# GpSimd's first task of a slot: the split of the probabilities or the integer sum of the lesser scores

## The chip, the cores and the metric

The kernel runs on one core of a Trainium2 chip. The metric is the device time of one execution in microseconds (us). The core has five engines that run their own instruction streams in program order and meet at semaphores: TensorE (PE in the profile; PEld is its loading of weights), VectorE (DVE), ScalarE (ACT), GpSimd (POOL) and the sync engine (SP), which here only issues transfers. Working memory is SBUF, and TensorE's results land in PSUM.

## The reference

Two blocks follow each other. The first is attention that keeps the 32 largest scores of a row; the second is a feed-forward block whose activation is h·cos(h). All is float32.

```python
# q, k, v: (8 batches, 8 heads, 576 tokens, 64)
scores = scale * q @ k.T
kth = np.partition(scores, -32, axis=-1)[..., -32:-31]
scores = np.where(scores >= kth, scores, -1e9)
attn = np.exp(scores - scores.max(-1, keepdims=True))
attn = attn / (attn.sum(-1, keepdims=True) + 1e-9)
x = (attn @ v) as (4608 tokens, 512)
h = x @ w_in            # 512 -> 2048
out = (h * np.cos(h)) @ w_out   # 2048 -> 512
```

## The kernel before

**Units and slots.** The attention is cut into 144 units. A unit is 128 tokens and one pair of heads, so a tile of scores is 128 × 2 × 576. The main loop (line 849) has one slot for each unit, and a slot works on several units at once: `u` is the unit whose largest scores are searched, `w` the one before it (masking and exponentials), `x` the one before that (its probabilities are sent away to be transposed), and `z`, in even slots only, the two units before those, whose probabilities are multiplied with the values. Slots 0 to 8 follow `early_slot`, slots 9 to 140 `slot`, the rest `last_slot`. The order in which the functions are called is the order of the instructions on each engine: it is written by hand, and no scheduler moves anything.

**The search.** VectorE finds the 32 largest of 576 scores with MAX8 (line 349) and MATCH_REPLACE8 (line 354), eight at a time. To halve the work, the row is folded. `fold_high` (VectorE, line 244) takes the larger of each of 288 pairs into `rest`. The lesser of each pair comes from GpSimd: `fold_sum` (line 262) adds the two as integers into `low`, and `fold_low` (line 271) subtracts the larger one. Four rounds search `rest`, and then two rounds search `low`. There is one buffer `low`, so the integer sum of a slot has to wait until the last search of the slot before is over. That search stands at the end of a slot, interleaved with the sum (line 396) and the reciprocal (line 401) of the unit `w`; the reciprocal, `rden`, is VectorE's last instruction in a slot. In this document a slot starts where this reciprocal ends.

**Sending the probabilities.** ScalarE masks and exponentiates the scores of `w` in place (lines 380 and 388). A slot later, `send` (line 739) takes them as `x`. `split` has GpSimd copy the float32 words as two rows of 16-bit halves into the single buffer `halves` (line 421), and then the 16-bit halves of `rden`, 64 times each (line 423). `write_halves` (line 431) writes the buffer to DRAM, and `transposes` (line 437) reads it back transposed as `pT`; both are issued by the sync engine, whose queue also carries the loads of q, k, v and of weights.

**Using them.** In even slots `values` (line 474) has TensorE multiply two units' `pT` with the values. ScalarE copies the result to `xT` (line 481), and `scale_values` (line 493) has VectorE multiply `xT` by the transposed `rden` that came along in `pT`, one instruction for each of the two units. Both inputs of it are in SBUF. It stands ahead of the last search of `low`.

**The feed-forward block** is cut into small steps that are fed in between: products with `w_in` (line 539), the range reduction of the cosine's argument on GpSimd (lines 575 and 584, in even slots), the sine on ScalarE (line 594), the product h·cos(h) on GpSimd (line 601, in odd slots) and products with `w_out` (line 614). In the first slots the weights are also rebuilt from 64-bit input: lines 138 and 151 on GpSimd and line 141 on VectorE.

GpSimd's order in a full slot is thus: lines 262, 421, 423, 271, and then 601 in odd slots or 575 and 584 in even ones.

Of the kernel before, what the change touches and what calls it, by code (L numbers as in the profile page):

```python
# [30 lines left out]
def kernel(  # L31
# [52 lines left out]
    for i in range(DF // CW):  # L84
        w = consts.tile([P, NC, CW], F32, tag=f"w_in{i}", name=f"w_in{i}")
# [4 lines left out]
    for f in range(NF):  # L90
        w = consts.tile([P, DM], F32, tag=f"w_out{f}", name=f"w_out{f}")
# [146 lines left out]
    def fold_high(u):  # L238

        s, sc = u["s"], u["sc"]  # L240
        if u["n"] > EARLY:
            del u["sc"]
        u["rest"] = work.tile([P, 2, S], F32, tag="rest", name="rest", bufs=1)
        nc.vector.tensor_tensor(  # L244
            out=u["rest"][:, :, HS:S], in0=sc[:, :, 0:HS], in1=s[:, :, HS:S], op=ALU.max
        )

    def fold_now(u):

        s, sc = u["s"], u.pop("sc")  # L250
        u["low"] = work.tile([P, 2, HS], F32, tag="low", name="low", bufs=1)
        nc.vector.tensor_tensor(
            out=u["low"], in0=sc[:, :, 0:HS], in1=s[:, :, HS:S], op=ALU.min
        )

    def fold_sum(u):

        if not u["folds"]:
            return
        s = u["s"].bitcast(I32)  # L260
        u["low"] = work.tile([P, 2, HS], F32, tag="low", name="low", bufs=1)
        nc.gpsimd.tensor_tensor(  # L262
            out=u["low"].bitcast(I32), in0=s[:, :, 0:HS], in1=s[:, :, HS:S], op=ALU.add
        )

    def fold_low(u):

        if not u["folds"]:
            return
        low = u["low"].bitcast(I32)  # L270
        nc.gpsimd.tensor_tensor(  # L271
            out=low, in0=low, in1=u["rest"][:, :, HS:S].bitcast(I32), op=ALU.subtract
        )
# [15 lines left out]
    def topk_first(u, w):  # L289

        u["top"] = tops[u["n"] % len(tops)]
        merges = w and w["folds"]
        if merges:
            merge_first(w)
        if u["folds"]:
            if u["n"] > EARLY:
                fold_sum(u)
            fold_high(u)
        else:
            u["rest"] = work.tile([P, 2, S], F32, tag="rest", name="rest", bufs=1)  # L300
        if merges:
            merge_second(w)
        if u["folds"] and u["n"] <= EARLY:
            fold_now(u)
        topk_round(u, 0, [lambda: bounds(w), lambda: distances(w)] if w else ())

    def topk_round(u, rnd, between=(), ahead=None):
        top, rest, lasts = u["top"], u["rest"], TOPK // 8 - 1
        end = TOPK - 1 - 8 * rnd
        at = top[:, :, end : end - 8 if rnd < lasts else None : -1, 0]  # L310
        if u["folds"]:
            search(
                at, rest[:, :, HS:S] if rnd == 0 else rest[:, :, 0:HS], rest[:, :, 0:HS], rnd < lasts,
                between if rnd < lasts else (),
            )
        else:
            search(at, u["s"] if rnd == 0 else rest, rest, rnd < lasts, between)
        if rnd < lasts:
            return
        del u["rest"]  # L320
        if u["folds"]:
            low = u.pop("low")
            for k in range(TOPK // 16):
                more = k < TOPK // 16 - 1
                if ahead and not more:
                    scale_values(ahead)
                search(
                    top[:, :, 1 + 8 * k : 9 + 8 * k, 1], low, low, more,
                    () if more or rnd < lasts else between,
                )  # L330
# [3 lines left out]
    def merge_first(u):  # L334
        n = TOPK // 2 + 1
        u["lesser"] = u["top"].rearrange("p j r i -> p j (r i)")[:, :, 2 * n : 3 * n]
        nc.vector.tensor_reduce(
            out=u["lesser"], in_=u["top"][:, :, 0:n], axis=mybir.AxisListType.X, op=ALU.min
        )

    def merge_second(u):
        nc.vector.tensor_reduce(
            out=u["top"][:, :, TOPK - 1, 1], in_=u.pop("lesser"), axis=mybir.AxisListType.X,
            op=ALU.max,
        )
# [10 lines left out]
    def bounds(u):  # L356

        top = u.pop("top").rearrange("p j r i -> p j (r i)")
        end = 2 * TOPK
        if not u["folds"]:  # L360
            nc.vector.tensor_copy(out=top[:, :, end - 1], in_=top[:, :, 0])
        less = u["less"] = top[:, :, end : end + 2]
        u["near"] = top[:, :, end - 1 : end + 1]
        nc.vector.tensor_reduce(
            out=less, in_=top[:, :, end - 2 : end].unsqueeze(3), axis=mybir.AxisListType.X,
            op=ALU.max, negate=True,
        )

    def distances(u):
        u["nd"] = small.tile([P, 2], F32, tag="nd", name="nd")  # L370
        nc.vector.tensor_reduce(
            out=u["nd"], in_=u.pop("near"), axis=mybir.AxisListType.X, op=ALU.add
        )
# [42 lines left out]
    def split(u):  # L416


        s = u.pop("s").rearrange("p j k -> p (j k)").bitcast(U16)
        halves = work.tile([P, 2, 2 * S + P], U16, tag="halves", name="halves", bufs=1)  # L420
        nc.gpsimd.tensor_copy(out=halves[:, :, 0 : 2 * S], in_=s.rearrange("p (k h) -> p h k", h=2))  # L421
        rden = u.pop("rden").bitcast(U16).rearrange("p (j h) -> p h j", h=2)
        nc.gpsimd.tensor_copy(
            out=halves[:, :, 2 * S :].rearrange("p h (j d) -> p h j d", j=2),
            in_=rden.unsqueeze(3).to_broadcast([P, 2, 2, D]),
        )
        u["halves"] = halves

    def write_halves(u):
        rows = u["rows"] = dram.tile([P, 2, 2 * S + P], U16, tag="rows", name="rows")  # L430
        nc.sync.dma_start(out=rows, in_=u.pop("halves"))

    def transposes(u):
        rows = u.pop("rows").rearrange("q h k -> (q h) k")
        pT = u["pT"] = work.tile([P, 2 * NT + 2, P], F32, tag="pT", name="pT", bufs=3)
        words = pT.rearrange("p c q -> p (c q)").bitcast(U16)
        nc.sync.dma_start_transpose(
            out=words.rearrange("p (c q) -> p c q", c=2 * NT + 2), in_=rows
        )
# [121 lines left out]
    def take_banks():  # L561
        while full:
            take, *what = full.popleft()
            take(*what)
# [22 lines left out]
    def sines(least):  # L587

        n = sum(c[3] < ff["now"] for c in waiting)
        if n == 0 or (n < least and waiting[0][3] + 2 > ff["now"]):  # L590
            return
        for _ in range(n):
            blk, g, x, _ = waiting.popleft()
            nc.scalar.activation(out=x, in_=x, func=AF.Sin, bias=halfpi, scale=TWO_PI_BELOW)  # L594
            sined.append((blk, g, x))
# [143 lines left out]
    def send(x):  # L739

        split(x)
        write_halves(x)
        transposes(x)

    def slot(i, u, w, x, z):
        load_weights(2)
        topk_first(u, w)
        if x:
            send(x)
        fold_low(u)  # L750
        topk_round(u, 1)
        topk_round(u, 2)
        made = scored.get(i, [])
        if z:
            take_banks()
        feed(1)

        ahead = i < EARLY + 5 * NP
        if z and not ahead:
            values(z)  # L760
        for m in made:
            scores(m)
        if z and ahead:
            values(z)


        late = len(made) > 0

        decoding = i < EARLY + 8
        if i % 2 and not decoding:  # L770
            sines(1)
        if w:
            mask(w)
        take_banks()
        if w and late:
            exponentials(w)
        if z and not ahead:
            take_values(z)
        take_scores(units[i + 1])
        if z and ahead:  # L780
            take_values(z)
        if w and not late:
            exponentials(w)
        decode_second(2)
        topk_round(u, 3, both(w), z)
        for load, b, hp in at_slot.get(i, []):
            load(b, hp)
        gate(1)
        feed(1 if len(made) == 2 else 2)
        take_banks()  # L790
        decode_third()
        decode_first(2)
        reduce_first()
        reduce_second()
        feed(1 if len(made) == 2 else 3)
        if decoding or i == LAST:
            sines(1)
# [51 lines left out]
    for i in range(NU + 1):  # L849
# [4 lines left out]
        u, w = (units[i - n] if 0 <= i - n < NU else None for n in range(2))  # L854
# [55 lines left out]
```

## Time and profile before

| what | value |
|---|---|
| time, median of 3 runs | 1515.53 us (1513.83 to 1517.55) |
| span of the profiled execution | 1510.3 us |
| granted TensorE clock, mean of the span | 0.972 |
| GpSimd, integer sum L262, each of 133 | 1413 ns |
| GpSimd, split L421, each of 132 | 2106 ns |
| GpSimd, rden copy L423, each of 132 | 406 ns |
| GpSimd, subtraction L271, each of 133 | 1415 ns |
| GpSimd, range reduction L575 and L584, each of 68 | 1050 ns and 2363 ns |
| VectorE, scaling of the values L493, each of 132 | 476 ns |
| issue to landing, rows written | 3.0 us |
| issue to landing, transposes | 5.1 us |

Durations are means of one instruction, and the two landings are medians. The page gives for every group of instructions the time that its engine was busy with it, the mean of one, and how long the engine stood idle just before, with the instruction that ended the idle time. Idle time of an engine costs nothing by itself. What matters is whether another engine, in the end, stood waiting for it.

### The profile page before, as it was taken

Reading aid. Unit: us, or ns where it says so; the run is one execution under the profiler, and the core shown is the slowest. Engines: PE = TensorE matmul, PEld = TensorE weight load, DVE = VectorE, ACT = ScalarE, POOL = GpSimd, SP = SyncE. Lnnn points to the kernel's source line nnn. Section 1 sums busy time; section 2 is a strip of 40 time slices with the busy share of each in tenths; the row PEclk is TensorE's granted clock in tenths of the full one; section 3 lists DMA queues with packets and bytes.
Section 4 is the critical chain, followed back from the end, with each engine's and each line's share of the span. In section 5 each row is a group of like instructions: output and inputs, shape, how many; then the busy total and the mean of one; then the engine's idle time right before and its main releaser. Section 6 shows DMA issues by size and latency. Waiting matters only on the chain.

```text
span 1510.3 us, 30568 instructions
## 1 busy us (share of the span) xinstructions
PE 1414.7 (94%) x10360; PEld 1014.2 (67%) x10360; DVE 1392.2 (92%) x5209; ACT 1093.4 (72%) x1974; POOL 1157.2 (77%) x836
## 2 busy tenths in 40 slices
PE   4778799999999999999999999999999999999999
PEld 3556567766777766766667767676676766677665
DVE  7999989999999999999999999999899999999831
ACT  4667667777777777777777777777677776777641
POOL 4779878888888887888888888888788888888410
PEclk6689999999999999999999999999999999999999
DMA  8534666567555666556655566557655556645200
GB/s 275 150 106 123 153 183 179 141 161 194 162 160 144 158 189 167 154 143 187 178 151 141 147 188 166 159 147 192 161 163 148 146 155 170 160 135 146 78 8 14
DMA packets 405549, 229.54 MB, mean 152 GB/s; under 512 B 355088, under 2 KB 371728, under 8 KB 405392
## 3 DMA queue, kind: packets, MB, share of 16 engines
q1 hardware_dynamic: 399984, 217.93, 53.2%
q10 hardware_dynamic: 5408, 9.65, 1.8%
q8 instruction: 82, 1.34, 0.4%
q14 instruction: 75, 0.61, 0.1%
HBM read 45.09 MB, written 95.94 MB: 93 GB/s over the span
## 4 chain that ended last, share of the span: by engine, by line
PE 39%; DVE 36%; DMA 10%; ACT 9%; POOL 3%; issue 2%; SPq 1%; ACTq 0%; POOLq 0%
DVE top L349 17%; PE mm L539 14%; PE o L614 13%; DVE rest L354 10%; DMA pT<-rows 7%; PE rim L474 5%; PE sc L223 4%; DVE rest L244 3%; DVE low L354 3%; ACT s L388 2%; DVE xT L493 2%; ACT L388 1%; ACT s L233 1%; PE rim L223 1%; DMA v<-in_v_dram 1%
## 5 line engine op out<-in xcount | busy, mean ns | idle before, releaser
L539 PEld LDWEIGHTS mm<-xT,w_in 128*128 128x128 f32 x4608 | 540.1, 193 | 68.6 <-issue 60.7
L614 PE MATMUL o<-w_out,g 128*128 128x512 f32 x1152 | 541.2, 603 | 12.7 <-POOL g L601 8.8
L539 PE MATMUL mm<-xT,w_in 128*128 128x128 f32 x4608 | 542.8, 276 | 0.9 <-DVE xT L493 0.5
L349 DVE MAX8 top<-rest 128x8 f32<-128x288 f32 x1148 | 481.4, 454 | 0.0
L354 DVE MATCH_REPLACE8 rest<-top,rest 128x288 f32<-128x288 f32 (+1 forms) x860 | 377.1, 446 | 0.0
L262 POOL TENSOR_TENSOR low<-s 128x576 int32<-128x576 int32 x133 | 187.9, 1413 | 214.7 <-DVE rden L401 205.0
L614 PEld LDWEIGHTS o<-w_out,g 128*128 128x128 f32 x1152 | 203.5, 191 | 200.4 <-issue 179.4
L421 POOL COPY halves<-s 128x2304 uint16<-128x2304 uint16 x132 | 277.9, 2106 | 0.1
L349 DVE MAX8 top<-low 128x8 f32<-128x288 f32 x568 | 239.4, 447 | 3.1 <-POOL low L271 3.0
L388 ACT ACTIVATE s<-s,nd 128x576 f32<-128x576 f32 x288 | 220.1, 767 | 0.8
L380 ACT ACTIVATE s<-s,top 128x576 f32<-128x576 f32 x288 | 206.0, 764 | 0.0
L474 PE MATMUL rim<-pT,v 128*64 128x128 f32 (+1 forms) x2560 | 164.4, 273 | 37.3 <-DMA pT<-rows 28.1
L474 PEld LDWEIGHTS rim<-pT,v 128*64 128x64 f32 x2560 | 133.5, 141 | 91.4 <-DMA pT<-rows 30.6
L271 POOL TENSOR_TENSOR low<-low,rest 128x576 int32<-128x576 int32 x133 | 188.2, 1415 | 0.2
L223 PE MATMUL sc<-k,q 64*128 64x448 f32 (+1 forms) x640 | 157.0, 588 | 11.0 <-DMA k<-in_k_dram 11.0
L584 POOL TENSOR_TENSOR x<-g,x 128x1024 f32<-128x1024 f32 x68 | 160.7, 2363 | 5.7
L553 ACT ACTIVATE g<-mm 128x512 f32<-128x512 f32 x144 | 84.9, 589 | 109.8 <-PE mm L539 107.7
L601 POOL TENSOR_TENSOR g<-g,x 128x1024 f32<-128x1024 f32 x68 | 161.4, 2374 | 2.7 <-ACT x L594 2.6
L481 ACT COPY xT<-rim 128x256 f32<-128x256 f32 (+1 forms) x78 | 27.9, 357 | 171.9 <-PE rim L223 148.6
L233 ACT COPY s<-sc 128x896 f32<-128x896 f32 x144 | 130.2, 904 | 5.2 <-PE sc L223 4.8
L354 DVE MATCH_REPLACE8 low<-top,low 128x288 f32<-128x288 f32 x284 | 123.6, 443 | 0.0
L244 DVE TENSOR_TENSOR rest<-sc,s 128x576 f32<-128x576 f32 x142 | 106.2, 748 | 6.8 <-ACT s L234 6.8
(59 smaller groups left out, 1401.7 us busy)
## 6 DMA issues: line engine op xcount, KB each, us to landing
rows<-halves SPq DMA_DIRECT2D x132, 640.0 KB, 3.0
out_dram<-ob ACTq DMA_DIRECT2D x36, 256.0 KB, 3.8
q<-in_q_dram SPq DMA_DIRECT2D x31, 288.0 KB, 3.5
st<-in_moe_w_in_dram SPq DMA_DIRECT2D x16, 512.0 KB, 5.6
v<-in_v_dram SPq DMA_DIRECT2D x32, 256.0 KB, 3.1
st<-in_moe_w_out_dram SPq DMA_DIRECT2D x16, 512.0 KB, 4.2
k<-in_k_dram SPq DMA_DIRECT2D x31, 144.0 KB, 3.5
k<-in_k_dram SPq DMA_DIRECT2D x32, 128.0 KB, 3.4
```

The lines of the kernel that those rows point to most:

```text
L223: nc.tensor.matmul(to[r0 : r0 + rows, j, 0 : k1 - k0], st["q"][d, q0 : q0 + rows], st["k"][d, k0:k1], start=True, stop=True,)
L262: nc.gpsimd.tensor_tensor(out=u["low"].bitcast(I32), in0=s[:, :, 0:HS], in1=s[:, :, HS:S], op=ALU.add)
L271: nc.gpsimd.tensor_tensor(out=low, in0=low, in1=u["rest"][:, :, HS:S].bitcast(I32), op=ALU.subtract)
L349: nc.vector.max(to[:, j], src[:, j])
L354: nc.vector.match_replace(rest[:, j], to[:, j], src[:, j], NEG)
L380: nc.scalar.activation(out=s[:, j], in_=s[:, j], func=AF.Prelu, bias=less[:, j, 1:2], scale=1.0, alpha=FAR)
L388: nc.scalar.activation(out=s[:, j], in_=s[:, j], func=AF.Exp, bias=nd[:, j : j + 1], scale=SCALE, accum_out=den[:, j, 0:1],)
L421: nc.gpsimd.tensor_copy(out=halves[:, :, 0 : 2 * S], in_=s.rearrange("p (k h) -> p h k", h=2))
L474: nc.tensor.matmul(o[d, to], lhsT, rhs, start=c == 0, stop=c == NT)
L539: nc.tensor.matmul(mm[:, at : at + w], w_in[f // FC][:, c, (f % FC) * P : (f % FC + 1) * P], blk["xT"][:, c], start=c == 0, stop=c == NC - 1,)
L601: eng.tensor_tensor(out=g, in0=g, in1=x, op=ALU.mult)
L614: nc.tensor.matmul(o, g[:, at : at + P], w_out[f], start=f == 0, stop=f == NF - 1)
```

## The change

The integer sum and the sending of the probabilities change places at the start of `slot`. Nothing is added or removed; every engine has the same instructions, and only GpSimd's stand in another order. The purpose is that GpSimd can start on the split, which doesn't need the buffer `low`, while VectorE is still searching that buffer.

```diff
     def slot(i, u, w, x, z):
         load_weights(2)
-        topk_first(u, w)
         if x:
             send(x)
+        topk_first(u, w)
         fold_low(u)
         topk_round(u, 1)
         topk_round(u, 2)
```

`topk_first` holds the integer sum (through `fold_sum`), `fold_high` and the first round of the search. On GpSimd the order in a slot becomes 421, 423, 262, 271.

## Prediction

> **What bounds the kernel now.** I read the busy shares first, then the waits of the whole span, then one pair of slots in the timeline, since work repeats every two slots.
>
> ```profile
> PE 1414.7 (94%) x10360; PEld 1014.2 (67%) x10360; DVE 1392.2 (92%) x5209; ACT 1093.4 (72%) x1974; POOL 1157.2 (77%) x836
> ```
>
> TensorE and VectorE are both nearly full; GpSimd is not. The shares decide nothing yet: two engines can bound in turn.
>
> ```profile
> POOL low L262 <- DVE rden L401: 205.0, 124, 4.5
> ...
> DVE xT L493 <- ACT xT L481: 33.8, 18, 5.5
> ...
> PE rim L474 <- DMA pT<-rows: 28.1, 24, 3.0
> ...
> DVE den L396 <- ACT s L388: 20.2, 23, 7.4
> ```
>
> Columns: total us, times, longest. GpSimd waits 1.65 us per slot (205.0/124) ahead of the integer sum, until VectorE's last search of the previous slot frees the single buffer `low`; that is the hole the change fills. TensorE's only large wait in mid-kernel is for transposed probabilities (pT).
>
> The pair of slots that starts at 836.4 us (end of the reciprocal L401) is one without a VectorE wait:
>
> ```profile
> 844.74 0.19 ACT L388 ACTIVATION_READ_ACCUMULATOR s<-s,nd 128x1 f32 x1
> ...
> 845.40 0.15 DVE L401 RECIPROCAL rden<-den 128x2 f32<-128x2 f32 x1
> 845.65 1.41 POOL L262 TENSOR_TENSOR low<-s 128x576 int32<-128x576 int32 x1 [1.62 <-DVE rden L401]
> ...
> 847.00 2.11 POOL L421 COPY halves<-s 128x2304 uint16<-128x2304 uint16 x1
> ...
> 849.04 0.41 POOL L423 COPY halves<-rden 128x256 uint16<-128x256 uint16 x1
> ...
> 849.41 1.42 POOL L271 TENSOR_TENSOR low<-low,rest 128x576 int32<-128x576 int32 x1
> ...
> 850.79 1.05 POOL L575 TENSOR_SCALAR x<-x 128x1024 f32<-128x1024 int32 x1
> 851.93 2.37 POOL L584 TENSOR_TENSOR x<-g,x 128x1024 f32<-128x1024 f32 x1
> ...
> 853.60 1.04 DVE L493 TENSOR_TENSOR xT<-xT,pT 128x128 f32<-128x128 f32 x2
> ...
> 855.36 0.14 DVE L401 RECIPROCAL rden<-den 128x2 f32<-128x2 f32 x1
> ```
>
> The odd slot lasts 9.12 us (836.43 to 845.55), the even one, which holds the two multiplications L493, 9.95 us (to 855.50): 19.05 us per pair. Below, T is the start of a slot (end of L401). L493 starts at T+8.05 and its two instructions take 1.04 us, because GpSimd's L584 runs until T+8.75:
>
> ```profile
> L493 DVE TENSOR_TENSOR xT<-xT,pT x132: 276/285/956, 152.4 to 1423.7; 128x128 f32<-128x128 f32 x132
> ```
>
> Alone it takes about 0.28 us (min/median/max). By the ends of L401, the 63 pairs from 174.9 to 1402.5 us average 19.49 us; what exceeds 19.05 (27.5 us in all) are the waits on xT and on ScalarE above, late pT or late k behind many. TensorE by itself could go faster: the chain of waits has the first products with the values at
>
> ```profile
> 1161.33 2.33 PE rim L474 x40
> ...
> 1180.03 2.34 PE rim L474 x40
> ...
> 1198.72 2.33 PE rim L474 x40
> ```
>
> so 18.69 us per pair while it catches up. VectorE sets the pace, TensorE is 2% behind that.
>
> **What the Trainium skill says.** "SBUF — State Buffer", § Who interferes with whom: a VectorE instruction with two SBUF inputs contends with a GpSimd instruction that reads SBUF, one with at most one SBUF input and outside the two-port modes does not. The trace agrees: L493 (two SBUF inputs) is stretched beside L584, while L244 (one input in PSUM) takes 0.75 us beside L262, its mean on the page. Same section: whoever issues first holds the shared pair for the whole instruction and the other blocks fully. L141, 0.42 us alone, took 1.415 us when it began inside a split (first lines below), so the split blocks too.
>
> **The change, part by part.** Same instructions on every engine; only GpSimd's order in a slot with a split moves, from sum, split, rden copy, subtraction to split, rden copy, sum, subtraction.
>
> (1) The split no longer waits for `low`. It needs the exponentials of its unit, finished in the slot before, and the landing of the previous halves. The rows write was issued at T+3.9 and landed 3.0 us later (median on the page), long before. No new wait comes from there.
>
> (2) Before an even slot GpSimd then waits for the exponentials: 844.93, or T−0.62, and 0.1 us of wake-up as seen before L262. Split T−0.52 to +1.58, rden copy to +1.93, sum to +3.31, subtraction to +4.68, L575 to +5.70, L584 to **T+8.15** instead of +8.75. The search of `low` comes at about T+6.4, so an earlier subtraction is worth nothing there.
>
> (3) The write of the halves starts 2 us earlier in even slots (rden copy done at +1.93, was +3.90). In odd slots the split can start in the slot before, so rden is what it waits for: done at about T+0.5 to +1.3 for +3.9. pT lands 2 to 3 us earlier; the longest TensorE wait on it was 3.0 us. That wait nearly goes.
>
> (4) The cost. In an even slot GpSimd used to idle from T+8.75 to the end. Now **the next slot's split follows L584 at once**, at T+8.1, and reads SBUF for 2.1 us, exactly where VectorE stands at L493 (request T+8.05). Its inputs are ready: exponentials of that unit ended at 850.47, T+4.9. The first L493 waits 0.1 us for L584 and should go next; the second then competes with the split. The trace has the same meeting:
>
> ```profile
> 146.56 2.09 POOL L421 COPY halves<-s 128x2304 uint16<-128x2304 uint16 x1
> 147.53 1.95 DVE L141 TENSOR_SCALAR w_out<-w_out 128x512 int32<-128x512 int32 x2
> 148.60 0.59 POOL L423 COPY halves<-rden 128x256 uint16<-128x256 uint16 x1
> ...
> 114.14 0.76 DVE L141 TENSOR_SCALAR w_out<-w_out 128x512 int32<-128x512 int32 x2
> 114.22 2.88 POOL L601 TENSOR_TENSOR g<-g,x 128x1024 f32<-128x1024 f32 x1 [1.27 <-ACT x L594]
> ```
>
> At 147.53 VectorE was blocked first. The split ended at 148.65, one L141 ran, then the rden copy (done 149.19), then the second L141 (149.48): they alternate. Two other blocked pairs (126.30 and 136.59 us) alternate too. At 114.14 VectorE was first, kept the port for both, and L601 was the one to wait (2.88 for 2.37). Here VectorE is blocked first, so I take alternation: L493 ends when the split does, T+8.15+0.13+2.06, plus 0.1: T+10.45. If L421 gets in before the first L493 (L584 ends before 8.05, or xT comes late), both wait for it and the end is the same within 0.1 us. Against T+9.10 now, VectorE loses 1.35 us in every even slot. Behind L493 on VectorE stand the last search of `low`, the sum and the reciprocal, hence the next slot: nothing hides it. Bounds: 0.55 us gained (VectorE keeps the port, L493 done at 8.55) to 1.6 us lost.
>
> (5) The sum. A pair becomes 19.05+1.35 = 20.40 us. TensorE (18.69) and the waits on pT, k and ScalarE fit inside it, so the 27.5 us of waits go, but each pair costs more than today's average: 63 × (20.40−19.49) = +57 us. Four TensorE-heavy pairs (20.5 us, units of two batches) add 1 us. The slots before 174.9 and the tail, where TensorE is last, stay. 1515.5+58 = **1573 us**.
>
> **Rivals.** *A, the port lets both L493 pass* (chance 0.17): VectorE needs 19.05−0.55 = 18.50 per pair, pT is early, TensorE becomes the bound at its floor. Between its starts at 211.8 and 1394.6 us 61 pairs took 1182.8 us; at 18.69, 18.85 for two-batch units and 20.45 for the heavy ones they would take 1146, so 37 us less; I leave 4 for k loads: 1482 us. For it: the pairs at 114 and at 152 us, where VectorE kept the port. Against it: there GpSimd came second, and as soon as xT is late by 0.1 us the split is first.
>
> *B, some of both* (0.11): the port blocks half of the pairs, and TensorE's floor holds in the others: (20.40+18.69)/2 = 19.55, that is 63×0.06 = +4 us: 1519 us, with any mixture from 1500 to 1555.
>
> *My forecast* (0.72): 1573 us; a loss of 1.1 to 1.6 us per even slot gives 1557 to 1589.
>
> *Transfers instead*: the earlier writes could meet loads on the sync queue. The queue's transposes end 2 us before the next write in either order, so I give this no case of its own.
>
> **Range and chances.** 1500 to 1590 holds nearly all of the forecast and of B, leaving out A and a little above. Faster is A and a sixth of B: 0.19; same 0.03; slower 0.78.
>
> **What would show it.** Right: L493's median rises from 285 ns, with one of the two near 2 us in most pairs; the wait of L262 on rden nearly gone; TensorE's waits on something later than VectorE, its idle up by about 1.5 us per pair; waits of DVE on xT nearly gone; L244 still 748 ns. A would show L493 near 0.3 us and pairs of 18.7 us. Wrong in step (2) if L584 doesn't end near T+8.15; wrong in (4) if the second L493 runs ahead of the split.

## The result and the profile after

| | before | changed |
|---|---|---|
| time, median of 4 runs | 1516.54 us | 1568.09 us |
| ratio to before, 95% interval | | 1.033 (1.030 to 1.037) |
| span of the profiled execution | 1510.3 us | 1566.3 us |
| 63 pairs of slots (those that end at 1402.5 us before) | 1227.6 us | 1283.1 us |
| scaling of the values L493, both instructions of an even slot together (mean) | 0.95 us | 2.35 us |

The change makes the kernel 3.3% slower; the forecast was 1573 us. The page after begins with the busy time of each engine; below it stand the engines' shares of the chain of work that ended last, after and then before:

```profile
PE 1427.7 (91%) x10360; PEld 1015.5 (65%) x10360; DVE 1483.3 (95%) x5209; ACT 1097.7 (70%) x1974; POOL 1167.6 (75%) x836
...
DVE 81%; PE 9%; ACT 4%; issue 2%; DMA 2%; POOL 1%; SPq 1%; ACTq 0%; POOLq 0%
...
PE 39%; DVE 36%; DMA 10%; ACT 9%; POOL 3%; issue 2%; SPq 1%; ACTq 0%; POOLq 0%
```

VectorE has the same instructions and is busy 91 us longer (1392.2 before). Its share of the chain that ends last went from 36% to 81%. The scaling of the values alone accounts for the 91 us. Its group reads (busy us, mean ns, then idle time), before and after:

```profile
L493 DVE TENSOR_TENSOR xT<-xT,pT 128x128 f32<-128x128 f32 x132 | 57.6, 476 | 34.3 <-ACT xT L481 33.8
...
L493 DVE TENSOR_TENSOR xT<-xT,pT 128x128 f32<-128x128 f32 x132 | 149.8, 1173 | 7.5 <-ACT xT L481 7.4
```

The minimum, median and maximum of one such instruction after the change, in ns:

```profile
L493 DVE TENSOR_TENSOR xT<-xT,pT x132: 277/326/2187, 152.4 to 1481.4; 128x128 f32<-128x128 f32 x132
```

Of the 66 even slots, 57 have a second scaling of over 2 us; before, no scaling took over 0.96 us. The median hides it, since a little over half of the 132 instructions are still short. The list of waits (total us, times, longest) shows that what the change aimed at did happen:

```profile
POOL halves L421 <- ACT s L388: 178.7, 63, 3.7
...
POOL halves L423 <- DVE rden L401: 69.2, 63, 2.2
...
PE mm L539 <- DVE xT L493: 43.6, 31, 2.6
...
DVE xT L493 <- ACT xT L481: 7.4, 2, 5.5
...
PEld rim L474 <- DMA pT<-rows: 1.5, 2, 0.8
```

The wait of the integer sum on rden fell from 205.0 to 1.3 us. TensorE's own wait on pT, 28.1 us before, is no longer listed; its weight load has 1.5 us. In their place TensorE waits for the scaling, 43.6 us. An even slot, from the end of L401 at 860.14 to that at 871.49, in the timeline:

```profile
861.63 0.40 POOL L423 COPY halves<-rden 128x256 uint16<-128x256 uint16 x1
...
866.01 2.37 POOL L584 TENSOR_TENSOR x<-g,x 128x1024 f32<-128x1024 f32 x1
...
868.21 2.42 DVE L493 TENSOR_TENSOR xT<-xT,pT 128x128 f32<-128x128 f32 x2
868.30 2.18 POOL L421 COPY halves<-s 128x2304 uint16<-128x2304 uint16 x1
...
871.35 0.14 DVE L401 RECIPROCAL rden<-den 128x2 f32<-128x2 f32 x1
...
880.43 0.15 DVE L401 RECIPROCAL rden<-den 128x2 f32<-128x2 f32 x1
```

L584 ends at 868.38, T+8.24. The first scaling starts at 868.21, is stretched to 0.32 us and finishes; the split L421, which has followed L584 at once, runs until 870.48; the second scaling, from 868.44 on, ends just after it at 870.63, T+10.49. The slot takes 11.35 us (9.95 before), the odd one after it 9.09. This repeats almost everywhere at 20.43 us per pair.

Two kinds of place in the same trace can be set against this. The last even slot before the end of `slot` has no split behind its L584, because `last_slot` sends later:

```profile
1456.57 2.36 POOL L584 TENSOR_TENSOR x<-g,x 128x1024 f32<-128x1024 f32 x1
1458.76 0.52 DVE L493 TENSOR_TENSOR xT<-xT,pT 128x128 f32<-128x128 f32 x2
1460.00 0.14 DVE L401 RECIPROCAL rden<-den 128x2 f32<-128x2 f32 x1
```

Both scalings together take 0.52 us there, and that pair of slots takes 18.53 us. In three pairs GpSimd is 1 us early, so that the split is there first:

```profile
579.93 2.37 POOL L584 TENSOR_TENSOR x<-g,x 128x1024 f32<-128x1024 f32 x1
582.23 2.12 POOL L421 COPY halves<-s 128x2304 uint16<-128x2304 uint16 x1
583.10 1.60 DVE L493 TENSOR_TENSOR xT<-xT,pT 128x128 f32<-128x128 f32 x2
```

Here the first scaling waits for the rest of the split (1.40 us) and the second takes 0.28 us, since the copy of rden that comes next isn't ready.

### The profile page after: what moved, and what is told of

It reads as the page before. It is cut to its first block, busy times and chain, and to the rows that moved or that the text cites. A ratio compares the mean times of both kernels' runs of the same rounds, so it can differ in the third digit from the quotient of the medians.

```text
span 1566.3 us, 30505 instructions
## 1 busy us (share of the span) xinstructions
PE 1427.7 (91%) x10360; PEld 1015.5 (65%) x10360; DVE 1483.3 (95%) x5209; ACT 1097.7 (70%) x1974; POOL 1167.6 (75%) x836
## 3 DMA queue, kind: packets, MB, share of 16 engines
q10 hardware_dynamic: 5408, 9.65, 1.7%
## 4 chain that ended last, share of the span: by engine, by line
DVE 81%; PE 9%; ACT 4%; issue 2%; DMA 2%; POOL 1%; SPq 1%; ACTq 0%; POOLq 0%
DVE top L349 35%; DVE rest L354 21%; DVE xT L493 9%; DVE low L354 6%; DVE rest L244 6%; PE mm L539 3%; PE o L614 3%; PE rim L474 2%; DMA v<-in_v_dram 1%; DVE top L337 1%; ACT s L388 1%; ACT s L380 1%; DVE den L396 1%; DVE top L342 1%; PE tp L448 1%
## 5 line engine op out<-in xcount | busy, mean ns | idle before, releaser
L539 PE MATMUL mm<-xT,w_in 128*128 128x128 f32 x4608 | 553.4, 277 | 55.2 <-DVE xT L493 43.6
L421 POOL COPY halves<-s 128x2304 uint16<-128x2304 uint16 x132 | 281.5, 2132 | 178.9 <-ACT s L388 178.7
L262 POOL TENSOR_TENSOR low<-s 128x576 int32<-128x576 int32 x133 | 187.9, 1413 | 1.3 <-DVE rden L401 1.3
L378 ACT ACTIVATE nd<-nd 128x2 f32<-128x2 f32 x144 | 29.3, 204 | 217.3 <-DVE nd L371 217.1
L584 POOL TENSOR_TENSOR x<-g,x 128x1024 f32<-128x1024 f32 x68 | 160.5, 2361 | 5.7
L223 PE MATMUL sc<-k,q 64*128 64x448 f32 (+1 forms) x640 | 152.7, 590 | 8.5 <-DMA k<-in_k_dram 8.5
L493 DVE TENSOR_TENSOR xT<-xT,pT 128x128 f32<-128x128 f32 x132 | 149.8, 1173 | 7.5 <-ACT xT L481 7.4
```

What stands on the lines that cost most here:

```text
L262: nc.gpsimd.tensor_tensor(out=u["low"].bitcast(I32), in0=s[:, :, 0:HS], in1=s[:, :, HS:S], op=ALU.add)
L493: nc.vector.tensor_tensor(out=to, in0=to, in1=u.pop("pT")[:, 2 * NT + 1], op=ALU.mult)
L539: nc.tensor.matmul(mm[:, at : at + w], w_in[f // FC][:, c, (f % FC) * P : (f % FC + 1) * P], blk["xT"][:, c], start=c == 0, stop=c == NC - 1,)
```

## The experiments

The theory: the loss is the meeting of the split and the scaling at the SBUF port, and the early sending by itself is a gain. Its rivals: the later integer sum, the moved transfers or the sending ahead of the sum as such cost the time. All times below stand against the kernel before on the same chip (1516.54 us for the first four, 1517.39 us for the last four).

| kernel | us | ratio to before (95%) |
|---|---|---|
| e1: changed order, scaling from PSUM | 1465.68 | 0.967 (0.964 to 0.969) |
| e2: order of before, scaling from PSUM | 1497.45 | 0.987 (0.984 to 0.990) |
| e3: changed order in even slots alone | 1486.53 | 0.981 (0.977 to 0.985) |
| e4: changed order in odd slots alone | 1607.55 | 1.060 (1.057 to 1.063) |
| e7: changed order, one scaling for two | 1468.17 | 0.970 (0.966 to 0.973) |
| e8: control for e7 | 1568.57 | 1.036 (1.031 to 1.040) |
| e5: changed, rden copied first | 1498.11 | 0.989 (0.985 to 0.993) |
| e6: e5 with scaling from PSUM | 1470.62 | 0.971 (0.968 to 0.974) |

### e1 and e2: the meeting taken away, under either order

```diff
     def take_values(us):
...
-        nc.scalar.copy(out=to, in_=room[0][:, 0 : n * P])
+        if not us[0]["paired"]:
+            nc.scalar.copy(out=to, in_=room[0][:, 0 : n * P])
...
     def scale_values(us):
-        for u in us:
+        for i, u in enumerate(us):
             to = block_of[u["tok"]]["xT"][:, u["hp"]]
-            nc.vector.tensor_tensor(out=to, in0=to, in1=u.pop("pT")[:, 2 * NT + 1], op=ALU.mult)
+            got = room[0][:, i * P : (i + 1) * P]
+            nc.vector.tensor_tensor(out=to, in0=got, in1=u.pop("pT")[:, 2 * NT + 1], op=ALU.mult)
```

> The order of the changed kernel, but the scaling of the values (one instruction for each of two units, VectorE) takes its first input straight from PSUM, so it has one SBUF input, and ScalarE's copy to xT is left out for paired units. GpSimd's order and the transfers are those of the changed kernel. Theory (the split that follows L584 at once holds the SBUF port that the second scaling needs): the scaling falls from 1.17 us mean to under 0.4 us, a pair of slots from 20.43 us to TensorE's floor of 18.7 us, the time to 1478 to 1490 us. Rival (the loss comes from the later integer sum or from transfers that now meet others): the time stays within 1% of 1568 us, with the scaling short and new waits on low or on transfers.

> The order of the kernel before, with the same scaling from PSUM as in e1. Theory: the 0.55 us for which L584 held up the scaling in most pairs go, so VectorE could do 18.5 us per pair and TensorE's 18.7 us binds; the probabilities still leave at T+3.9 us, so TensorE's waits on pT stay (about 0.25 us per pair): 1482 to 1495 us, some us slower than e1. Rival (what VectorE loses at the port in the kernel before is hidden by the waits on pT): 1510 us or more.

Measured: 1465.68 us for e1, 12 us below its range, and 1497.45 us for e2, 2 us above its range. (e1's range rests on the same floor of TensorE as rival A of the prediction; what that left out is said under Rivals.) With the two added lines the scaling is line 495. The trace of e1 gives for this line (minimum, median and maximum in ns), and for TensorE's products with the values between 700 and 780 us (start, duration):

```profile
L495 DVE TENSOR_TENSOR xT<-rim,pT x132: 271/281/292, 150.9 to 1377.9; 128x128 f32<-128x128 f32 x132
```

```profile
713.19 2.34 PE rim L474 x40
731.88 2.33 PE rim L474 x40
750.57 2.33 PE rim L474 x40
769.27 2.33 PE rim L474 x40
```

The scaling never exceeds 0.29 us, although GpSimd's order is that of the changed kernel, and TensorE's starts are 18.69 us apart: TensorE is now the bound (83% of the chain). So neither the later sum nor the moved transfers can have cost the 52 us: both are still there. What went is the long scaling, and with it ScalarE's copy to `xT`; e7 below keeps that copy and comes within 3 us of e1. e2 has the same short scaling and the old order, and keeps the waits on the transposes, as these lines of its waits show:

```profile
DVE xT L495 <- ACT s L234: 33.1, 17, 4.8
...
PE rim L474 <- DMA pT<-rows: 18.3, 15, 3.3
```

e1 has 1.2 us where e2 has 18.3. The difference of the two runs, 1497.45−1465.68 = 32 us, is what early sending is worth when the scaling can't be held. e1 beats both kernels.

### e3 and e4: each kind of slot alone

Against the changed kernel:

```diff
-        if x:
+        if x and i % 2 == 0:      # e3; e4 has 1 for 0, here and below
             send(x)
         topk_first(u, w)
+        if x and i % 2 != 0:
+            send(x)
```

> The change in even slots alone: there the split stands ahead of the integer sum; in odd slots the sum is first as before. The scaling is that of the kernel before. Theory: no split follows L584 within the even slot, so the scaling meets only the end of L584 (about 0.3 us each); a pair takes VectorE 18.5 us, TensorE 18.7 us, pT of odd slots leaves as late as before: 1482 to 1500 us. Rival (splitting first is what costs, in either slot): slower than before, about half of the loss, 1540 us.

> The change in odd slots alone. L584 in even slots then ends at T+8.75 us as in the kernel before, and the next slot's split follows it at once. Theory: the first scaling waits for L584 until 8.75, the second for the split until about 11.0, 1.9 us later than in the kernel before: a pair takes 21.0 us, the time is 1600 to 1620 us, slower than the full change. Rival (each slot's reordering costs its share): about 1540 us, between the two kernels.

Measured: 1486.53 and 1607.55 us, both inside what the theory gave. The same reordering in one kind of slot alone gains 2% or loses 6%, by where the split lands. In e3 the group of the scaling reads (busy us, mean ns, then idle time)

```profile
L493 DVE TENSOR_TENSOR xT<-xT,pT 128x128 f32<-128x128 f32 x132 | 38.3, 329 | 22.1 <-ACT xT L481 21.6
```

against a mean of 476 ns before: in the median L584 ends at T+8.27 for +8.74, and no split follows it. In e4 L584 is as late as before, and the split behind it as well:

```profile
863.60 2.35 POOL L584 TENSOR_TENSOR x<-g,x 128x1024 f32<-128x1024 f32 x1
865.29 2.92 DVE L493 TENSOR_TENSOR xT<-xT,pT 128x128 f32<-128x128 f32 x2
865.90 2.17 POOL L421 COPY halves<-s 128x2304 uint16<-128x2304 uint16 x1
```

The first scaling waits for L584, the second for the split. Pairs take 20.93 us, or 21.69 us where VectorE also waits for ScalarE's exponentials (0.7 us), which the expectation didn't have.

### e7 and e8: one scaling for two

```diff
     def transposes(u):
...
-        pT = u["pT"] = work.tile([P, 2 * NT + 2, P], F32, tag="pT", name="pT", bufs=3)
+        if u["n"] % 2 == 0:
+            both_pT[0] = work.tile([P, 2, 2 * NT + 2, P], F32, tag="pT", name="pT", bufs=2)
+        pT = u["pT"] = both_pT[0][:, u["n"] % 2]
+        u["pair"] = both_pT[0]
...
     def scale_values(us):
+        u = us[0]
+        to = block_of[u["tok"]]["xT"][:, u["hp"] : u["hp"] + 2]
+        nc.vector.tensor_tensor(out=to, in0=to, in1=u["pair"][:, :, 2 * NT + 1], op=ALU.mult)
         for u in us:
-            to = block_of[u["tok"]]["xT"][:, u["hp"]]
-            nc.vector.tensor_tensor(out=to, in0=to, in1=u.pop("pT")[:, 2 * NT + 1], op=ALU.mult)
...
```

with `XB` 3 for 4 (buffers x); e8 is the changed kernel with `XB` 3 alone.

> The changed kernel with the two scalings of an even slot made into one instruction of 256 elements (the two units' transposed probabilities lie in one buffer, two such buffers for three single ones, and the feed-forward block has three buffers x for four to make room). Still two SBUF inputs, same place on VectorE, same order on GpSimd. Theory (the two engines take turns at the port, one instruction each): the one scaling waits for the end of L584 alone and goes ahead of the split; it takes about 0.6 us, a pair of slots TensorE's 18.7 us, the time is 1466 to 1490 us. Rival (the split, once it follows L584, keeps the scaling out whatever its number): the scaling takes over 2 us, the time stays at 1560 us or more.

> Control for e7: the changed kernel with three buffers x for four and nothing else. Both theories: x is used by one step in two slots and lives for less than three pairs, so the time stays within 0.5% of the changed kernel, 1560 to 1576 us. If it moves by more, the gain of e7 is to be read against this run.

Measured: 1468.17 us for e7, 1568.57 us for e8, so the number of buffers x has no part in it. The buffers pT, two pairs for three single ones, had no run of their own; the changed kernel waited for pT for 1.5 us in all (above), so they had little to give. One instruction that still reads two SBUF inputs, at the same place in VectorE's order, regains 100 us (e8, on the same chip, against e7). Its place in the trace of e7 (L591 is L584, L498 the scaling):

```profile
869.10 2.36 POOL L591 TENSOR_TENSOR x<-g,x 128x1024 f32<-128x1024 f32 x1
871.29 0.45 DVE L498 TENSOR_TENSOR xT<-xT,pT 128x256 f32<-128x256 f32 x1
871.41 2.30 POOL L421 COPY halves<-s 128x2304 uint16<-128x2304 uint16 x1
```

VectorE asks first and passes, and this time it is the split that is held, 2.30 us for 2.10. (The changed kernel shows the same on a smaller scale: its split takes 2.17 us in the median where a scaling of 128 elements goes ahead of it.) Of 66 scalings three took over 1 us. So the split doesn't shut VectorE out; the two engines take turns here, and a second instruction of VectorE pays for a whole split. Whether turns are the rule, or the engine that asked first goes first, is open: in the slot of the changed kernel shown above, the split's record begins at 868.30 and that of the second scaling at 868.44, so both rules give the same order, and neither explains the two pairs of the prediction, at 114 and 152 us, in which VectorE went twice in a row.

### e5 and e6: sending ahead of the sum, but no split before the slot

The two copies in `split` change places, so that the one which waits for rden comes first:

```diff
+        nc.gpsimd.tensor_copy(out=halves[:, :, 2 * S :]..., in_=rden...)
         nc.gpsimd.tensor_copy(out=halves[:, :, 0 : 2 * S], in_=s.rearrange("p (k h) -> p h k", h=2))
-        nc.gpsimd.tensor_copy(out=halves[:, :, 2 * S :]..., in_=rden...)
```

> The changed kernel with the two copies of the split exchanged: the copy of rden, which has to wait for VectorE's reciprocal, stands ahead of the copy of the probabilities, so no split can start before the next slot does. Sending still stands ahead of the integer sum. Theory: L584 ends at about T+8.9 us and the port is free afterwards, so the scaling costs what it cost in the kernel before (first 0.85 us, second 0.28 us) and a pair takes 19.1 to 19.2 us without waits; the halves leave 1.3 us sooner than before, so most waits on pT go: 1488 to 1500 us, faster than before. Rival (sending ahead of the sum is what costs): near 1568 us.

> e5 with the scaling from PSUM as in e1. Theory: as the port doesn't matter to it any more and the probabilities leave early enough, TensorE's 18.7 us per pair binds and the time is that of e1, 1463 to 1475 us; up to 10 us more if 1.3 us of head start isn't enough for pT. Rival (e1 owes its gain to the split that runs in the slot before): 1485 us or more, near e2's 1497 us.

Measured: 1498.11 and 1470.62 us. In e5 sending still stands ahead of the sum, and the kernel is 1.1% faster than before. Its group of the scaling:

```profile
L493 DVE TENSOR_TENSOR xT<-xT,pT 128x128 f32<-128x128 f32 x132 | 71.6, 581 | 11.7 <-ACT xT L481 11.4
```

The scaling is 0.1 us longer in the mean than before the change, for only L584 is in its way: the usual pair has 0.92 to 0.95 and 0.28 us and takes 19.14 us. e6 is within 5 us of e1 (which ran on another chip): with the scaling short, halves that are done at T+2.5 for T+3.9 before reach TensorE nearly soon enough, and the split need not run in the slot before.

## Why the prediction was right, and where it was off

**(1), no new wait.** Right: the split waits for the exponentials in even slots (178.7 us over 63 waits) and 0.2 us in all for the halves' landing.

**(2), L584 at T+8.15.** Measured T+8.22 in the median. The estimate of a wake-up and six durations in a row was 0.07 us short.

**(3), pT earlier.** Right: the rden copy ends at T+0.46 in odd slots and T+1.89 in even ones (forecast 0.5 to 1.3, and 1.93).

**(4), the cost.** Right in kind and size. The scalings end at T+10.48 in the median, forecast T+10.45, and the long one is the second in 57 of 66 slots. Once (236 us) the first scaling came 0.2 us late and the split was ahead of both, as foreseen. That the engines would alternate was a likeness, not a deduction: it rested on three blocked pairs in the trace of before against two in which VectorE kept the port, and all but one of these five were pairs of L141, which has one SBUF input where L493 has two. One of the two pairs against was also misread: at 152 us the record of GpSimd's L151 begins first (152.32, that of L493 at 152.36), and yet L151 was held, so the order of the records doesn't settle who gets the port when they lie so close. e7 shows by experiment that the likeness held. The statement of the Trainium skill, "SBUF — State Buffer", § Who interferes with whom, that a VectorE instruction with at most one SBUF input, outside the two-port modes, doesn't contend with GpSimd agrees with e1's scaling (0.28 us) and with L244, 748 ns beside L262 and 747 ns beside L421. The port itself stands in no trace: the runs show who is held, and for how long.

**(5), the sum.** Forecast 1286 us for the 63 pairs, measured 1283.1. A usual pair takes 20.43 us (20.40). The term for four TensorE-heavy pairs (+1 us) was wrong: three of them took 19.5 us, for there the exponentials come 1 us earlier, the split is first, and L493 ends at T+9.65. The last pair, at 18.53 us, has no split behind it, which the sum hadn't allowed for. These lower the sum by about 5 us; 0.03 us in each usual pair and two longer early ones give some 3 back. Outside the 63 pairs the profile moves little, as assumed: the start is 2.1 us longer (174.9 to 177.0), the end 1.6 us shorter (107.8 to 106.2). The profiled spans differ by 56.0 us; the medians, whose runs before spread from 1513.83 to 1523.41, by 51.6.

**Rivals.** B did not occur: no usual pair fell to TensorE's 18.69 us. A did not occur either, but e1 is its world: TensorE is the bound there. A's time, 1482 us, was 16 us above e1's 1465.68, though its 61 pairs were nearly right: 1146 us, and 1144.0 in e1 between the same starts. What A left out is that the slots around these pairs get shorter too, by 3.7 us at the start and 5.0 at the end; the 4 us kept for loads of k were not needed, and the rest is the distance between medians and profiled executions (e1's medians gain 51 us, its spans 47.5). e1 differs from A also in leaving out ScalarE's copy; what the end slots owe to that was not separated.

**Signs named ahead.** TensorE's new waits come in every second pair: 2.7 us there, of which 1.5 us on L493 and the rest on ScalarE. Over the 63 pairs its idle time rose from 30.8 to 75.3 us, 0.7 us per pair where 1.5 was named. That 1.5 didn't fit the forecast's own sum, in which a pair grows by 0.91 us with the same work for TensorE. The median of L493 rose only from 285 to 326 ns, so as a sign it was badly chosen: where one of two instructions is long, the maximum and the count tell it.

## What to carry to other kernels

Before filling an idle stretch of GpSimd, look at what VectorE does in that stretch: here an instruction of VectorE with two SBUF inputs paid for a whole GpSimd instruction that stood in its way, and the idle time was what had kept it short. Two cures worked, to take one input from PSUM and to merge neighbours into one instruction, and neither gives up the better order: with the cure, the reordering that cost 3.3% is part of a kernel 3.3% faster than before. An edit that moves nothing on VectorE still cost time there, and it showed as longer instructions, not as waits.

## What the runs showed of the hardware

I had expected the first of two blocked scalings to go ahead, but not how regular the turns are: first VectorE, then the split, then VectorE, in 57 of 66 even slots (second scaling 2.18 us, alone 0.28). With a single instruction of 256 elements the median is 448 ns beside the same split. The record of the held scaling covers its wait; no idle time stands before it, and the list of waits doesn't name it.
